# Windowed attention and MoE in one kernel: the first four head pairs turn their probabilities on TensorE, and the weight chunks arrive in the order of their use

## The chip, the cores and the metric

The kernel runs on one core of a Trainium2 chip. The metric is the device time of one execution in microseconds (us), the median of the runs. The engines are TensorE (PE; PEld is its weight load), VectorE (DVE), ScalarE (ACT), GpSimd (POOL) and SyncE (SP). DMAs are issued by SP, and after the change one by ACT too. A sequencer takes the instructions of its engine in program order.

## What is computed

Eight batches of eight heads with 512 local and 32 global tokens of head size 64. Local queries see the global keys and a band of keys around them; global queries see all 544 keys. The attention output, as 4608 tokens of 512 numbers, goes through one MoE layer:

```python
s_ll = scale * np.matmul(q_l, k_l.transpose(0, 1, 3, 2))
mask = np.abs(pos[:, None] - pos[None, :]) <= 32
s_l = np.concatenate([s_lg, np.where(mask, s_ll, -1e9)], axis=-1)
out_l = np.matmul(sm(s_l), np.concatenate([v_g, v_l], axis=2))
...
x = attn_out.transpose(0, 2, 1, 3).reshape(B * S, H * D)
h = np.maximum(x @ w_in, 0.0)
out = h * h @ w_out
```

## The kernel before

**Blocks and steps.** Tokens are worked on in 17 blocks of 256: 16 of local tokens, two for each batch, and a last one that holds all the global tokens. The MoE of a block takes eight steps; step m multiplies the block with 256 columns of the first weight (`gemm1`, line 380, two column halves j, each adding up four chunks of 128 rows), applies ReLU and square (`act1`, line 397, and `act2`), and multiplies the result with the 256 matching rows of the second weight (`gemm2`, line 424), one step later. The two PSUM tiles of `gemm1`, h0 and h1, have one buffer each, so the product of the next step cannot write h0 before `act1` has read it.

**Block 0 is special.** Its products run in plain float32 (two passes for each product on TensorE) on the weights as they come; from block 1 on, weights and tokens are split into a high and a low float32r part.

**Attention.** The local attention of a block is done in four head pairs s. For each pair: `scores` (line 146; sixteen products of 32 queries on 128 keys, into the two PSUM tiles sb), `softmax1` (line 201; four DVE instructions that add the mask and take the extreme), `softmax2` (line 219; four exponentials on ACT), `softmax3` (line 227; sums, reciprocal and scaling on DVE), `transposes` (line 233; one DVE instruction that transposes 32x32 squares), `av` (line 238; 40 products over 32 keys each, since the squares stay in their quadrant of partitions), and `x_evac` (line 263; copies into the tokens x, or xg for block 0). Every second pair, `g_scores` and `g_rest` do the scores of the global queries; the last copies them from sb to SBUF.

**The order** is written out by hand. Lines 542 to 595 are the prologue: loads, then the pairs 0 to 3 of block 0 and the scores of pair 4. The loop at line 596 then runs one MoE step and half a pair at a time. Products named `warm` (line 161) work on zeros, between the others. The prologue's loads go through one SP queue, with up to eight in flight.

**Weights.** They come as 32 chunks of 512 KB (`w_load`), as 64-bit floats, and are turned into float32 on the chip: `w_abs` on ACT (letter a, `w_first`), `w_shift` and `w_or` on DVE (letters b and c), and later the split, `w_split` on ACT and `w_low` on DVE (letter s). The table `PLAN` says with these letters what is done at the four places of each step; `w_need` (line 520) fills in what a step needs and the table has not done. Chunks 4m and 4m+1 belong to `gemm1` of step m, 4m+2 and 4m+3 to its `gemm2`. `LOOK` says how many chunks ahead a load is asked for. All chunks and the early loads of pairs share a pool of 33 buffers.

Of the kernel before, what the change touches and what calls it, by code (L numbers as in the profile page):

```python
# [16 lines left out]
P = 128  # L17
# [18 lines left out]
PLAN = [",,,", ",,,", ",,,", ",,,", ",,,", ",,,", ",,,", ",,,", "bca,bca,bca,bc", "a,abcbc,abc,abc", "as,abcbc,abc,abcs", "a,abcbc,abc,abcs", "as,abcbc,abc,abcs", "a,abcbc,abc,abcs", "aas,bc,bcs,bcss", "s,ss,ss,ss", "s,,s,ss", ",,s,s", "s,,s,", ",,s,s", "s,,s,", ",,s,s", "s,,s,s", ",,,"]  # L36
LOOK = 6
NFIRST = 5
VFIRST = 5
# [25 lines left out]
def attention_moe(  # L65
# [3 lines left out]
    vv: bass.AP,  # L69
    qg: bass.AP,  # L70
# [12 lines left out]
    p1 = ctx.enter_context(tc.tile_pool(name="p1", bufs=1))  # L83
    ps_h = ctx.enter_context(tc.tile_pool(name="ps_h", bufs=1, space=PSUM))
# [22 lines left out]
    def load_v(p):  # L107
        v = early(p, VC, "v") if p < VFIRST else pv.tile([P, 2, VC], F32, tag="v", name=f"v{p}")
        sp.dma_start(v, vv[p])
        pairs[p]["v"] = v  # L110
# [3 lines left out]
    def g_load(k):  # L114

        qr = p2.tile([P, P], F32, tag="qr", name=f"qr{k}")
        sp.dma_start(qr, qg[k // 4, k % 2])
        state["q", k] = qr
# [42 lines left out]
    def warm(n):  # L161
        h = ps_o.tile([P, 512], F32, tag="o0", name="warm") if "warm" not in state else state["warm"]
        state["warm"] = h
        z = sg[:, :, 544:]
        for _ in range(n):
            pe.matmul(h[:96, :192], z[:, 0], z, start=True, stop=True, skip_group_check=True)
# [70 lines left out]

    def av(p):
# [24 lines left out]
    def x_evac(p):  # L263
# [4 lines left out]
        if g == 0:  # L268
            ac.copy(xg[:, c, :64], v_at(0))
            ve.tensor_copy(out=xg[:, c, 64:128], in_=v_at(1))  # L270
            ac.copy(xg[:, c, 128:], src)
        else:
            xv = p2.tile([P, 2, 64], F32, tag="xv", name=f"xv{p}")
            ac.copy(xv[:, 0], v_at(0))
            ve.tensor_copy(out=xv[:, 1], in_=v_at(1))
            xh, xl = x[:, g % 2, c, 0], x[:, g % 2, c, 1]
            xv = xv.rearrange("p a n -> p (a n)")
            for cols, part in ((slice(0, 128), xv), (slice(128, 256), src)):
                ac.copy(xh[:, cols], part)
                ve.tensor_sub(xl[:, cols], part, f(xh[:, cols]))  # L280
# [91 lines left out]

    def win(ws, step, j, c):
        o = 256 * (c % 2) + 128 * j
        return ws[4 * step + c // 2][:, o : o + 128]

    def wout(ws, step, j):
        return ws[4 * step + 2 + j]
# [141 lines left out]
    def w_need(m):  # L520

        if m <= 8:
            while w_next["or"] < min(4 * m + 2, WCH):
                w_second()
                w_third()
        if 8 <= m < 16:
            while w_next["low"] < 4 * (m - 8) + 4:
                n = w_next["low"]
                w_chunk(True)
                assert w_next["low"] > n, (m, w_next, w_bufs, sorted(w_used)[-1:])  # L530

    def w_done(m):
        w_used.update(range(4 * m, 4 * m + 4))
        for i in (4 * m, 4 * m + 2):
# [18 lines left out]
    load_v(2)  # L553
    load_qk(4)
    w_fetch(3)
    load_v(3)
    sp.dma_start(con[:, 2 * SW :], consts[:, 2 * SW :])
    w_fetch(4)
    g_load(2)
    w_fetch(5)  # L560
    load_qk(5)
    w_fetch(6)
# [12 lines left out]
    warm(3)  # L575
    g_rest(1)
    for s in range(1, 4):
        softmax1(s)
        softmax2(s, 0)
        softmax2(s, 1)  # L580
        scores(s + 1)
# [175 lines left out]
```

## Time and profile before

| | us |
|---|---|
| median of three runs (lowest, highest) | 960.55 (960.12, 961.61) |
| the profiled execution, its own time | 959.55 |
| span of its profile, first to last instruction | 957.8 |
| TensorE busy in it | 937.4 (98%) |

The profile's times count from the first instruction. A row of the timeline has start, length, engine, line, operation, the tiles as out<-in, shapes and a count of merged instructions; in square brackets stands how long the engine had been idle, and what ended that. All instructions go through one helper, so that the line is always L58 and rows are told apart by their tiles. TensorE's float32 products show as two passes each.

### The profile page before, as it was taken

Reading aid. Unit: us, or ns where it says so; the run is one execution under the profiler, and the core shown is the slowest. Engines: PE = TensorE matmul, PEld = TensorE weight load, DVE = VectorE, ACT = ScalarE, POOL = GpSimd, SP = SyncE. Lnnn points to the kernel's source line nnn. Section 1 sums busy time; section 2 is a strip of 40 time slices with the busy share of each in tenths; the row PEclk is TensorE's granted clock in tenths of the full one; section 3 lists DMA queues with packets and bytes.
Section 4 is the critical chain, followed back from the end, with each engine's and each line's share of the span. In section 5 each row is a group of like instructions: output and inputs, shape, how many; then the busy total and the mean of one; then the engine's idle time right before and its main releaser. Section 6 shows DMA issues by size and latency. Waiting matters only on the chain.

```text
span 957.8 us, 28465 instructions
## 1 busy us (share of the span) xinstructions
PE 937.4 (98%) x12214; PEld 757.4 (79%) x12214; DVE 568.9 (59%) x1676; ACT 415.4 (43%) x1323; POOL 0.5 (0%) x5
## 2 busy tenths in 40 slices
PE   6999999999999999999999999999999999999997
PEld 4666688888888888888888888888888888888886
DVE  4578875655556655665556655565555655664442
ACT  4477644443344434444344434444444434433222
POOL 0000000000000000000000000000000000000000
PEclk9799999999999999999999999999999999999999
DMA  9891322233122312233222322233232223210000
GB/s 358 338 338 58 124 61 79 74 102 122 61 95 75 111 61 91 73 102 115 69 96 73 92 77 94 74 102 96 87 95 73 83 85 95 70 31 24 1 23 23
DMA packets 60191, 93.40 MB, mean 98 GB/s; under 512 B 10401, under 2 KB 35233, under 8 KB 60065
## 3 DMA queue, kind: packets, MB, share of 16 engines
q1 hardware_dynamic: 60064, 91.58, 28.8%
q8 instruction: 96, 1.57, 0.7%
q14 instruction: 31, 0.25, 0.1%
HBM read 82.12 MB, written 8.91 MB: 95 GB/s over the span
## 4 chain that ended last, share of the span: by engine, by line
PE 92%; ACT 3%; DVE 3%; issue 1%; DMA 1%; SPq 0%; ACTq 0%
PE h L58 40%; PE o L58 38%; PE sb L58 5%; PE ab L58 4%; PE va L58 4%; DVE wf L58 1%; ACT wf L58 1%; ACT r L58 1%; DVE ws L58 1%; DMA wr<-in_w_dram 1%; ACT prob L58 1%; DVE prob L58 0%; PE warm L58 0%; ACT ws L58 0%; ACT sg L58 0%
## 5 line engine op out<-in xcount | busy, mean ns | idle before, releaser
L58 PE MATMUL h<-x,ws 128*128 128x512 f32 (+1 forms) x2048 | 389.6, 343 | 2.3 <-DVE x L58 2.1
L58 PEld LDWEIGHTS h<-x,ws 128*128 128x128 f32 x2048 | 315.4, 188 | 61.0 <-ACT x L58 6.5
L58 PE MATMUL o<-ws,gh 128*128 128x512 f32 x1024 | 321.2, 395 | 0.0
L58 PEld LDWEIGHTS o<-ws,gh 128*128 128x128 f32 x1024 | 183.8, 188 | 39.7
L58 DVE TENSOR_TENSOR r<-h,r 128x256 f32<-128x256 f32 x256 | 106.9, 419 | 169.1 <-ACT r L58 169.1
L58 PE MATMUL o<-ws,gl 128*128 128x512 f32 x512 | 202.4, 395 | 0.0
L58 ACT COPY r<-h 128x256 f32<-128x256 f32 x256 | 94.7, 371 | 241.9 <-PE h L58 241.8
L58 DVE TENSOR_TENSOR gl<-r,gh 128x512 fp32r<-128x512 f32 x128 | 88.7, 693 | 87.8 <-ACT gh L58 87.8
L58 ACT CAST gh<-r 128x512 fp32r<-128x512 f32 x128 | 79.4, 620 | 113.1 <-DVE r L58 113.1
L58 PEld LDWEIGHTS o<-ws,gl 128*128 128x128 f32 x512 | 96.4, 188 | 22.6 <-DVE gl L58 0.2
L58 ACT ACTIVATE prob<-prob,st 128x128 f32<-128x128 f32 x256 | 100.5, 396 | 12.3 <-DVE st L58 12.2
L58 DVE SCALAR_TENSOR_TENSOR r<-r 128x512 f32<-128x512 f32 x128 | 88.5, 692 | 4.4
L58 PEld LDWEIGHTS va<-pts,v 32*64 32x64 f32 x2560 | 59.6, 133 | 27.4 <-issue 24.2
L58 PE MATMUL ab<-pts,v 32*64 32x64 f32 (+1 forms) x2560 | 69.2, 230 | 0.0
L58 PE MATMUL va<-pts,v 32*64 32x64 f32 (+1 forms) x2560 | 66.7, 229 | 2.4 <-issue 1.8
L58 DVE CUSTOM_DVE_ANT_0 prob<-sb,con 128x128 f32<-128x128 f32 x256 | 58.5, 284 | 8.2 <-PE sb L58 5.2
L58 PEld LDWEIGHTS ab<-pts,v 32*64 32x64 f32 x2560 | 58.5, 133 | 0.0
L58 ACT COPY xv<-va 128x64 f32<-128x64 f32 x60 | 12.7, 212 | 83.9 <-PE va L58 82.1
L58 ACT ACTIVATION_READ_ACCUMULATOR prob<-prob,st 128x1 f32 x256 | 48.6, 190 | 0.0
L58 PE MATMUL sb<-raw 64*32 64x128 f32 x2048 | 44.1, 278 | 3.8 <-DMA raw<-in_qk_dram 1.5
L58 DVE STREAM_TRANSPOSE pts<-prob 128x512 f32<-128x512 f32 x64 | 45.5, 711 | 2.5
L58 DVE TENSOR_TENSOR prob<-prob,st 128x512 f32<-128x512 f32 x64 | 44.3, 692 | 2.2
(50 smaller groups left out, 544.7 us busy)
## 6 DMA issues: line engine op xcount, KB each, us to landing
raw<-in_qk_dram SPq DMA_DIRECT2D x64, 480.0 KB, 4.9
v<-in_vv_dram SPq DMA_DIRECT2D x64, 320.0 KB, 3.6
wr<-in_w_dram SPq DMA_DIRECT2D x32, 512.0 KB, 8.7
gv<-in_vg_dram SPq DMA_DIRECT2D x32, 320.0 KB, 3.5
out_dram<-ot SPq DMA_DIRECT2D x32, 256.0 KB, 2.0
qr<-in_qg_dram SPq DMA_DIRECT2D x32, 64.0 KB, 4.9
xg<-xt SPq DMA_DIRECT2D x128, 4.0 KB, 1.8
out_dram<-ot SPq DMA_DIRECT2D x8, 64.0 KB, 1.7
```

What stands on the lines that cost most here:

```text
L58: r = method(*args, **kwargs)
```

## The change

**First four pairs.** Pairs 0 to 3 (`NTURN = 4`) no longer use `transposes`, `av` and `x_evac`. `turn` lets TensorE transpose the four 128x128 tiles of probabilities, by products with the identity, into one PSUM tile pt; `turn_evac` copies it to SBUF, one half on ACT and one on DVE; `turn_av` makes 16 products over 128 keys each, into h0 for even pairs and h1 for odd ones; `turn_x` copies the result on ACT. For that, the values of these pairs come in another layout (v1, 512 KB for each pair instead of 320 KB), in which the 128 partitions hold the 128 keys. The branch of `x_evac` for block 0 goes.

**Order of the phases.** The prologue is rewritten: the softmax of a pair starts before the one before it is scaled, the four pairs overlap, `g_scores(1)` comes late, and the scores of pair 4 and `g_scores(3)` stand behind the first `gemm1` instead of ahead of it. The value products of pair 3 stand right ahead of the first `gemm1`.

**Loads.** The first half of the masks is issued by ACT; the identity has a DMA of its own and comes early; two of the first weight chunks come later than before, the second half of the masks too. The query tiles of the global tokens get four buffers.

**Weights.** The chunks lie in memory in the order in which the steps use them (chunks 0 and 1 for `gemm1` of step 0, 2 and 3 for that of step 1, then the two of `gemm2` of step 0, and so on), `PLAN` has other letters in steps 8, 9, 14 and 15, `w_need` is asked ahead of each of the two products, and `LOOK` is 9 instead of 6.

```diff
-LOOK = 6
+LOOK = 9
+NTURN = 4
...
+    def turn(p):
+        if p == 0:
+            state["pt"] = ps_o.tile([P, 512], F32, tag="o1", name="pt")
+        for n in range(4):
+            pe.transpose(state["pt"][:, SW * n : SW * n + SW], probs[p % 2][:, n], ident)
+
+    def turn_evac(p):
+        pts = p1.tile([P, 4 * SW + 96], F32, tag="pts", name=f"pts{p}")
+        ac.copy(pts[:, : 2 * SW], state["pt"][:, : 2 * SW])
+        ve.tensor_copy(out=pts[:, 2 * SW : 4 * SW], in_=state["pt"][:, 2 * SW :])
+        pairs[p]["pts"] = pts
+
+    def turn_av(p):
+        d = pairs[p]
+        state["vt"] = ps_h.tile([P, 512], F32, tag=f"h{p % 2}", name=f"vt{p}")
+        for a in range(4):
+            for u in range(2):
+                for e in range(2):
+                    q = SW * (2 * e + u) + BLK * a
+                    o = 2 * BLK * a + BLK * u
+                    pe.matmul(
+                        state["vt"][half(e), o : o + BLK],
+                        d["v"][:, 2 * a + u, e],
+                        d["pts"][:, q : q + BLK],
...
+    def turn_x(p):
+        w_take(-1)
+        ac.copy(xg[:, p], state["vt"][:, :HALF])
...
+    def w_in(step):
+        return max(4 * step - 2, 0)
+
+    def w_out(step):
+        return min(4 * step + 4, WCH - 2)
...
+    ac.dma_start(masks[:, : 2 * SW], consts[:, : 2 * SW])
     load_qk(0)
-    sp.dma_start(masks[:, : 2 * SW], consts[:, : 2 * SW])
-    g_load(0)
     load_qk(1)
-    w_fetch(1)
     load_qk(2)
     load_v(0)
-    g_load(1)
+    sp.dma_start(ident, consts[:, 4 * SW :])
     load_qk(3)
-    w_fetch(2)
+    w_fetch(1)
+    g_load(0)
     load_v(1)
     load_v(2)
+    w_fetch(2)
+    load_v(3)
+    w_fetch(4)
     load_qk(4)
...
-    warm(4)
+    warm(16, 64)
     scores(0)
-    g_scores(0)
-    warm(2)
     softmax1(0)
     softmax2(0, 0)
     softmax2(0, 1)
+    warm(4)
     scores(1)
+    softmax1(1)
+    softmax3(0)
+    softmax2(1, 0)
+    softmax2(1, 1)
+    warm(1)
+    scores(2)
+    turn(0)
+    softmax1(2)
+    turn_evac(0)
+    softmax2(2, 0)
+    softmax2(2, 1)
+    turn_av(0)
+    softmax3(1)
+    scores(3)
     g_scores(1)
+    turn_x(0)
+    turn(1)
+    softmax1(3)
     w_first()
+    turn_evac(1)
+    softmax2(3, 0)
+    softmax2(3, 1)
...
+    softmax3(3)
+    turn(3)
+    turn_x(2)
+    w_first()
+    turn_evac(3)
+    warm(1)
+    w_third()
+    w_second()
+    w_third()
...
+        if t == LAG:
+            turn_av(s - 1)
+            turn_x(s - 1)
+            g_rest(1)
...
             gemm1(m, 0)
             gemm1(m, 1)
         run_jobs(t, "evac")
+        if t == LAG:
+            scores(s)
+            g_scores(s - 1)
+            w_tick(t, 0)
...
+        if m > 0:
+            w_need(m, 2)
```

On DVE, in the stretch where pair 1 is turned before the change: st and prob are the softmax's sums and probabilities, wf and wr weight chunks, xg the tokens of block 0, sb the scores.

```order
L58 TENSOR_SCALAR st_201<-st_201 128x4 [waits Activation_49]
L58 RECIPROCAL st_201<-st_201 128x4 [waits DVE_49]
L58 TENSOR_TENSOR prob_87<-prob_87,st_201 128x512 [waits DVE_49]
L58 STREAM_TRANSPOSE pts_320<-prob_87 128x512 [waits DVE_49,PE_49]
L58 TENSOR_SCALAR wf_194<-wf_194 128x512 [waits Activation_49]
L58 COPY xg<-va_1_324 128x64 [waits PE_49]
L58 SCALAR_TENSOR_TENSOR wf_194<-wr_109,wf_194 128x512 [waits DMAHW1_49,DVE_49]
```

On DVE after the change, from the copy of pair 1's transposed tile on, pairs 2 and 3 included (pt is the PSUM tile that TensorE transposes into):

```order
L59 COPY pts_306<-pt 128x256 [waits Activation_49]
L59 TENSOR_SCALAR st_238<-st_238 128x4
L59 RECIPROCAL st_238<-st_238 128x4 [waits DVE_49]
L59 TENSOR_TENSOR prob_89<-prob_89,st_238 128x512 [waits DVE_49]
L59 TENSOR_SCALAR wf_304<-wf_304 128x512
L59 COPY pts_340<-pt 128x256 [waits Activation_49]
L59 TENSOR_SCALAR st_299<-st_299 128x4
L59 RECIPROCAL st_299<-st_299 128x4 [waits DVE_49]
L59 TENSOR_TENSOR prob_90<-prob_90,st_299 128x512 [waits DVE_49]
L59 COPY pts_370<-pt 128x256 [waits Activation_49]
L59 SCALAR_TENSOR_TENSOR wf_304<-wr_107,wf_304 128x512 [waits DMAHW7_49]
```

The square transposes and the 64-column copies are gone, a copy of half of pt stands in their place and waits for ACT's copy of the other half, and the weight chunks' work has moved behind the pairs.

On ACT before the change, from the exponentials of pair 3 (x4) to the ReLU of the first product (r<-h):

```order
L58 ACTIVATE prob_87,st_376<-prob_87,st_376 128x128 x4
L58 COPY xg<-va_0_408 128x64
L58 COPY xg<-ab 128x128
L58 ACTIVATE wf_374<-wr_122 128x512
L58 COPY xg<-va_0_461 128x64
L58 COPY xg<-ab 128x128
L58 ACTIVATE prob_86,st_516<-prob_86,st_516 128x128 x2
L58 ACTIVATE wf_529<-wr_126 128x512
L58 ACTIVATE wf_529<-wr_130 128x512
L58 ACTIVATE r_536<-h_0_506 128x256
L58 ACTIVATE r_536<-h_1_511 128x256
```

On ACT after the change, from the last copies of the pairs to the same ReLU (sg holds the scores of the global queries, prob_89 the pair 4):

```order
L59 COPY pts_370<-pt 128x256
L59 COPY xg<-vt_377 128x256
L59 COPY sg<-sb_91 128x160
L59 COPY sg<-sb_92 128x128
L59 ACTIVATE wf_431<-wr_119 128x512
L59 ACTIVATE wf_431<-wr_121 128x512
L59 COPY sg<-sb_91 128x160
L59 COPY sg<-sb_92 128x128
L59 ACTIVATE prob_89,st_438<-prob_89,st_438 128x128 x2
L59 ACTIVATE wf_457<-wr_126 128x512
L59 ACTIVATE wf_457<-wr_128 128x512
L59 ACTIVATE r_466<-h_0_397 128x256
```

Between the last copy into xg and the ReLU there stood two exponentials and two weight chunks; now there are four copies of global scores, four chunks and the two exponentials, and the last two copies and the exponentials belong to scores that TensorE makes behind the first product.

More of the change, by code (lines that the diff above doesn't have):

```diff
@@ L69, in attention_moe @@
     vv: bass.AP,
+    v1: bass.AP,
     qg: bass.AP,
@@ L107, in load_v @@
     def load_v(p):
+        if p < NTURN:
+            w_take(1)
+            r = wp.tile([P, 1024], F32, tag="w", name=f"v{p}")
+            sp.dma_start(r, v1[p])
+            pairs[p]["v"] = r.rearrange("p (w e n) -> p w e n", w=8, e=2)
+            return
         v = early(p, VC, "v") if p < VFIRST else pv.tile([P, 2, VC], F32, tag="v", name=f"v{p}")
@@ L114, in g_load @@
     def g_load(k):
-        qr = p2.tile([P, P], F32, tag="qr", name=f"qr{k}")
+        qr = p4.tile([P, P], F32, tag="qr", name=f"qr{k}")
         sp.dma_start(qr, qg[k // 4, k % 2])
@@ L236, in transposes @@
         pairs[p]["pts"] = pts
+    def turn(p):
[20 more added lines that the diff above has]
+                        d["pts"][:, q : q + BLK],
+                        start=True,
+                        stop=True,
+                        skip_group_check=True,
+                    )
+    def turn_x(p):
+        w_take(-1)
+        ac.copy(xg[:, p], state["vt"][:, :HALF])
+        pairs[p]["v"] = None
     def av(p):
@@ L267, in x_evac @@
         src = ab[:, 448:576]
[L268 to L280, printed above, removed]
+        xv = p2.tile([P, 2, 64], F32, tag="xv", name=f"xv{p}")
+        ac.copy(xv[:, 0], v_at(0))
+        ve.tensor_copy(out=xv[:, 1], in_=v_at(1))
+        xh, xl = x[:, g % 2, c, 0], x[:, g % 2, c, 1]
+        xv = xv.rearrange("p a n -> p (a n)")
+        for cols, part in ((slice(0, 128), xv), (slice(128, 256), src)):
+            ac.copy(xh[:, cols], part)
+            ve.tensor_sub(xl[:, cols], part, f(xh[:, cols]))
         pairs[p]["v"] = None
@@ L571, in attention_moe @@
     softmax2(0, 1)
+    warm(4)
     scores(1)
+    softmax1(1)
[12 more added lines that the diff above has]
+    scores(3)
     g_scores(1)
+    turn_x(0)
+    turn(1)
+    softmax1(3)
     w_first()
[L575 to L581, printed above, removed]
-        g_scores(s + 1)
-        warm(1)
-        softmax3(s - 1)
-        transposes(s - 1)
-        w_second()
-        new_va(s)
-        av(s - 1)
-        x_evac(s - 1)
-        warm(3 if s < 3 else 1)
-        w_third()
-        g_rest(s + 1)
-        w_first()
-    softmax3(3)
-    transposes(3)
+    turn_evac(1)
+    softmax2(3, 0)
+    softmax2(3, 1)
+    warm(1)
+    turn_av(1)
+    softmax3(2)
+    turn(2)
+    turn_x(1)
+    w_second()
+    turn_evac(2)
+    warm(1)
+    turn_av(2)
+    softmax3(3)
+    turn(3)
+    turn_x(2)
+    w_first()
+    turn_evac(3)
+    warm(1)
+    w_third()
+    w_second()
+    w_third()
     for t in range(LAG, NSTEP + LAG + 1):
@@ L713 @@
             vv[:, hf, :, BLK * a : BLK * a + BLK, 4] = v_g
+    v1 = np.zeros((NTURN, P, 8, 2, D), f4)
+    for p in range(NTURN):
+        for a in range(4):
+            for u in range(2):
+                for slot in range(4):
+                    n = order[u][SHIFT[a] + slot]
+                    rows = slice(BLK * slot, BLK * slot + BLK)
+                    src = v_g if n == g else vb[:, :, u + n]
+                    v1[p, rows, 2 * a + u] = src[0, 2 * p : 2 * p + 2].transpose(1, 0, 2)
+    v1 = v1.reshape(NTURN, P, 16 * D)
     qk = np.ascontiguousarray(qk.reshape(NP, 2, P, QK).transpose(0, 2, 1, 3))
```

71 lines of the change are left out of this document (42 added, 29 removed).

## Prediction

> **What bounds the kernel now.** I read the page first, then the windows of the first 100 us, the timeline of TensorE there, the DMA queues, and for durations the groups of instructions.
>
> ```profile
> span 957.8 us, 28465 instructions
> PE 937.4 (98%) x12214; PEld 757.4 (79%) x12214; DVE 568.9 (59%) x1676; ACT 415.4 (43%) x1323; POOL 0.5 (0%) x5
> ...
> PEclk9799999999999999999999999999999999999999
> ```
>
> TensorE is busy for 98%, so only its early gaps, its early half clock and the moment when its dense work begins are left to win. The timeline of TensorE has them (here the rows of the big products and the long gaps):
>
> ```profile
> 1.04 2.87 PE L58 MATMUL warm<-sg 128*96 128x192 f32 x8 [1.04 <-POOL sg L138]
> ...
> 7.08 0.67 PE L58 MATMUL sb<-raw 64*32 64x128 f32 x32 [1.21 <-DMA raw<-in_qk_dram]
> 7.51 0.55 PE L58 MATMUL sb<-raw,qr 64*32 64x160 f32 x16
> ...
> 16.15 0.55 PE L58 MATMUL sb<-raw 64*32 64x128 f32 x23 [1.24 <-issue]
> ...
> 22.45 2.08 PE L58 MATMUL warm<-sg 128*96 128x192 f32 x6 [3.82 <-issue]
> ...
> 32.47 8.57 PE L58 MATMUL h<-xg,wf 128*128 128x256 f32 x32
> ...
> 46.34 3.72 PE L58 MATMUL h<-xg,wf 128*128 128x256 f32 x16
> ...
> 55.72 2.86 PE L58 MATMUL h<-xg,wf 128*128 128x256 f32 x12 [1.33 <-DVE wf L58]
> ...
> 72.38 2.86 PE L58 MATMUL h<-xg,wf 128*128 128x256 f32 x12 [0.25 <-DVE wf L58]
> ...
> 97.59 1.32 PE L58 MATMUL h<-x,ws 128*128 128x512 f32 x6
> 101.02 2.02 PE L58 MATMUL h<-x,ws 128*128 128x512 f32 x10 [2.11 <-DVE x L58]
> ```
>
> Dense work begins at 32.47 with the first two `gemm1` (32 passes), which end at 41.04. From there on TensorE is held up by three gaps of note, 1.33 + 0.25 + 2.11 = 3.7 us, the last in the first product of block 1, which starts at 97.59; all later work is the same before and after. So the end moves by two terms: how much earlier the second `gemm1` ends, and how much of the 3.7 us goes.
>
> Why does it begin only at 32.47? The windows tell:
>
> ```profile
> 16.10:18.70 2.60, 2.48 (x127) 2.00 (x128) 0.70 (x3) 0.17 (x2) 0.00 (x0) 1.00 1.06 398
> ...
> 18.70:21.60 2.90, 0.00 (x0) 0.02 (x1) 2.73 (x14) 2.71 (x13) 0.00 (x0) 1.00 1.02 398
> 21.80:35.20 13.40, 10.84 (x209) 8.03 (x209) 5.97 (x21) 3.51 (x11) 0.00 (x0) 0.50 1.03 404
> ```
>
> Counts up to the first gap, and DVE's work on the way to block 1:
>
> ```profile
> 0.00:15.50 15.50, 10.79 (x221) 7.70 (x221) 6.36 (x34) 8.07 (x31) 0.46 (x5) 1.00 0.89 335
> ...
> 28.60:97.60 69.00, 65.22 (x791) 44.10 (x790) 54.24 (x142) 46.10 (x121) 0.00 (x0) 0.95 0.61 228
> ```
>
> The queue of instruction fetches, in the window of 19 to 21 us and over the run (packets, MB, share):
>
> ```profile
> q8 instruction: 1, 0.02, 3.5%
> ...
> q8 instruction: 96, 1.57, 0.7%
> ```
>
> The columns of the windows are PE, PEld, DVE, ACT, POOL, the granted clock, the DMA share and GB/s. In the gap of 18.7 to 21.6 TensorE waits for nothing but "issue", with all DMA engines full. Between that gap and the one of 1.24 us it had issued 127 + 128 = 255 instructions. One packet of code came in 19 to 21 us; over the run 96 packets carry 1.57 MB, 16 KB each. So I read it that TensorE ran dry: its code arrives in blocks of about 256 instructions, behind a full queue of data. The Trainium skill (Runtime: NRT & Kernel Launch, section Instruction fetch mechanics) has the same 16 KiB blocks but calls the fetch hidden. By the page the change would win 1.0 us more than in the sum below; the gaps of 1.24 and 3.82 us here speak against it. After the long gap the clock stays at 0.50 until 35.3, and the first two products take 8.57 us instead of 2 x 3.72.
>
> **The change, term 1: when the second `gemm1` ends.** Durations first. From the chain of waits in order of time (start, length, what):
>
> ```profile
> 2.60 5.58 DMA wr<-in_w_dram
> ...
> 9.08 0.29 DVE prob L58
> ...
> 10.34 0.70 DVE prob L58
> 11.07 0.72 DVE pts L58
> 11.84 0.27 PE va L58
> ```
>
> The first and last row of pair 0's four exponentials on ACT:
>
> ```profile
> 5.49 0.40 ACT L58 ACTIVATE prob<-prob,st 128x128 f32<-128x128 f32 x1 [3.48 <-DVE st L58]
> ...
> 6.95 0.18 ACT L58 ACTIVATION_READ_ACCUMULATOR prob<-prob,st 128x1 f32 x1
> ```
>
> From the groups by form (count, busy us and mean ns), the nearest relatives of what is new, and a weight chunk's three steps:
>
> ```profile
> L58 ACT COPY r<-h 128x256 f32<-128x256 f32 x256 | 94.7, 371 | 241.9 <-PE h L58 241.8
> L58 DVE TENSOR_TENSOR r<-h,r 128x256 f32<-128x256 f32 x256 | 106.9, 419 | 169.1 <-ACT r L58 169.1
> L58 DVE COPY gp<-ab 128x128 f32<-128x128 f32 x1 | 0.3, 285 | 0.0
> L58 PE MATMUL ab<-con,sg 128*128 128x128 f32 x5 | 0.7, 273 | 0.0
> L58 PE MATMUL ab<-gv,gp 128*32 128x64 f32 x40 | 0.8, 222 | 0.0
> L58 ACT ACTIVATE wf<-wr 128x512 f32<-128x512 f32 x32 | 20.2, 667 | 1.1 <-DMA wr<-in_w_dram 1.1
> L58 DVE TENSOR_SCALAR wf<-wf 128x512 int32<-128x512 int32 x32 | 13.3, 415 | 10.0 <-ACT wf L58 10.0
> L58 DVE SCALAR_TENSOR_TENSOR wf<-wr,wf 128x512 int32<-128x512 int32 x32 | 22.2, 695 | 1.0
> ```
>
> A `softmax1` takes 0.9 us (9.08 to about 10.0), `softmax3` 1.1 us (to 11.05), a pair's exponentials 1.65 us (5.49 to 7.13). A turn is four transposes like the five of 0.7 us: 0.65. ACT's half of `turn_evac` is the 371 ns copy. DVE's half is shown by no row: between the 285 ns of half its size and the 419 ns of an add from PSUM I take 0.42, near the row of its own size. The value products, 32 passes over 128 keys, come nearest to the 40 passes of 0.8 us: 0.6; if every pass waited for a weight load, at the product's 3.72/16 = 0.23 us, they would be 7 us, which the products' 256 columns against 32 here speak against, so 1.7 at most. Loads: the first weight chunk landed at 8.18 with 1.70 MB up to it, 4.2 us at 404 GB/s, so a load lands 4.0 us after its bytes' time. In the new order that gives pair 1's queries and keys at 6.8, pair 2's at 8.0, values of pair 0 at 9.3 and of pair 3 at 17.3, the identity at 9.4, weight chunks 0 and 1 at 12.0 and 16.0. The larger values (192 KB more a pair) and the masks on ACT's queue are in these sums; no load ends up last.
>
> Step by step: the 32 small warm passes, a third of the 0.36 us row each, end at about 4.8, so the first scores (0.67 us each time) at 5.5. Pair 1's scores follow at 7.1 to 7.8, its `softmax1` at 7.9 to 8.8, pair 0's `softmax3` behind it on DVE until 9.9, `turn(0)` until 10.6. `softmax1(2)` writes the tile that is being turned, so it ends at 11.3, and DVE's half of `turn_evac(0)`, queued behind it, at 11.75; value products, scores 3 and `g_scores(1)` take TensorE to 13.45. Here its second wait for code falls. Counting four instructions a product and two a transpose, the 442 (221 + 221) that ran before the first gap are used up at the end of `g_scores(1)`. The next block is asked for in `scores(1)` at 7.4; after the gaps above it ran 6.3 us after the block before it had started (16.15 to 22.45), the first one 8.2 us (8.0 to 16.15). That gives 13.7 to 15.6: a wait of 0.2 to 2.2 us, I take 1.0. The block after that is asked for at 14.5 and needed at 26.
>
> From `turn(1)` at 14.5 the pairs run in a chain, each: turn 0.65, ACT's copy 0.4, then DVE's copy 0.42 (it waits for ACT's), `softmax3` of the next pair 1.1, handoffs 0.25, about 2.8 us; so `turn(2)` at 17.4, `turn(3)` at 20.15, its copies done at 21.7, its value products at 22.35. The first `gemm1` begins at 22.4 with chunk 0; chunk 1 is shifted and joined behind the last copy on DVE (0.61 + 0.43 + 0.61 of pitch) until 23.35, so the product ends at 26.15.
>
> Then a new wait. The scores of pair 4 and `g_scores(3)` hold TensorE to 27.3 (1.1 us that before lay ahead of 32.47). The second `gemm1` writes h0 and must wait for ACT's ReLU; and that is queued behind the copies of the global scores, which wait for `softmax1(4)` (27.75), two exponentials (28.85) and two weight chunks (29.95). It starts at 30.3 and ends at 34.0, against 41.04: **7.0 us**. Before, the clock's 1.2 us and the late start hid that queue.
>
> **Term 2: the gaps.** The two on wf came as DVE had not joined chunks in time. In the new order `gemm1` of step m needs 4m chunks, not 4m + 2, two chunks or 2.1 us of DVE less. The 2.11 us at 98.9 came as DVE joined the last two chunks ahead of the tokens of block 1; `PLAN` now does them in step 7. From 23.4 until block 1 begins, at about 89.6 (97.6 - 7.0 less 1.0 of gaps), DVE has 66 us for the 54.2 us of work that it did between 28.6 and 97.6. Asking nine chunks ahead keeps DMA full until about 67 us (25.1 MB up to the last chunk), where it was 0.61 busy on average. I keep 0.7 of the 3.7 us: **3.0 us**.
>
> Together 10.0 us: 959.55 becomes 949.5. The median of before lies 1.0 above its profiled execution, so I forecast 950.5. The bounds: no wait for code (-0.8), no gaps (-0.7), DVE's copies at 0.29 (-0.4), shorter queue on ACT (-0.8), first scores sooner (-0.3) make 947.5; the block of code late (+1.2), value products at 1.7 (+1.1 on the path, twice), half of the gaps back (+1.5) make 955.4.
>
> **Rivals.**
>
> *The clock drops* (0.2). TensorE's pairs have many short pauses and one of 3.0 us behind the first product. Before, the clock fell 3.0 us after the idle time began, and 10.84 busy us of 13.40 did not bring it back while the matmuls were small. If it falls in the prologue, each pair's scores, turn and values grow by about 0.7, and the first two products cost the 1.2 us again: 4.0 us, 954.5. Against it: until the long gap the clock stayed at 1.00 with gaps of up to 1.24 us. The Trainium skill (TensorE: Matmul & The Clock Gate, Part 1) lets the clock fall after an idle window of 3.4 us that runs free and raises it after a busy one; by that, an estimate from the page, the pause alone would cost nothing or up to 1.7 us. The trace agrees on the fall (3.0 us into the gap) and not on the rise.
>
> *DVE and ACT cannot follow* (0.15). If they wait as much as before (69 us for 54 us of work), block 1 begins at 23.4 + 69 = 92.4, 5.2 us earlier than before and no more, with its own gap as it was: 955.3. For it speaks the chain DVE, ACT, DVE of each chunk; against it that chunks now come earlier.
>
> *Slower: TensorE runs out of code among the small products of the loop* (0.04). A pair's 64 small products (40 + 16 + 8) use a whole block of 256 in 2 us, while a block takes 6.3 us under a full queue, and the queue is now full until 67 us. Should two boundaries fall into the same pair, each time 4.1 us are lost; three such pairs of the four make 12.3 us, 962.8 with all gains spent. The point is where the boundaries lie: by my count 1210 and 1466 enclose pair 5 and 8 us of work, so it decides only if a block takes over 8 us. In before no such gap showed after 32.47.
>
> *The code's wait only moves* (0.01): the first product would still come at 32, about 960.
>
> **How the numbers follow.** The forecast case has 0.60 and is 950.5, by itself 947.5 to 953; the range goes on to the rivals at 954.5 and 955.3 and the upper bound: 947.5 to 956. A measurement of this kernel can tell about 0.2% (1.9 us) from no change. Faster 0.95, same 0.01, slower 0.04.
>
> **What would show it.** Right: the first `gemm1` starting at 21.5 to 24 at clock 1.00; no "issue" gap over 2.2 us; a pause of about 3 us ahead of the second `gemm1`, ended by ACT's r; block 1's first product near 89.6 with under 1 us of gap. Wrong: a first product after 26, PEclk at 0.50 beyond 10 us, or gaps on wf or x that add up to 3.7 us again.

## The result, and the profile after

| | before | after |
|---|---|---|
| median of four runs each (lowest, highest), us | 960.34 (959.89, 961.61) | 949.40 (948.81, 950.44) |
| after / before, 95% interval | | 0.9885 (0.9868 to 0.9902) |
| profiled execution, its own time, us | 959.55 | 948.81 |
| end of the second `gemm1` | 41.03 | 35.37 |
| end of block 1's first product | 103.04 | 92.52 |
| end of TensorE's last product | 952.59 | 941.78 |

The changed kernel is 1.15% faster; 950.5 was forecast, 949.4 measured, inside the range. "Lead" below is how much earlier than before the same product ends: 5.66 us at the second `gemm1`, 10.53 at block 1's first product, 10.81 at the end. So the first term of the sum is 5.7 us (7.0 forecast) and the second 4.9 (3.0 forecast): the total holds because two misses, of 1.4 and 1.9 us, have opposite signs. That is luck.

The page of the changed kernel, in the lines that answer to those of before:

```profile
span 947.0 us, 28126 instructions
PE 933.7 (99%) x12048; PEld 756.3 (80%) x12048; DVE 567.2 (60%) x1672; ACT 416.5 (44%) x1323; POOL 0.5 (0%) x5
...
PEclk9999999999999999999999999999999999999999
```

The timeline of TensorE, in its rows with the turned pairs (pt: the transposes, vt: the value products) and the big products:

```profile
9.93 0.63 PE L59 MATMUL pt<-con,prob 128*128 128x128 f32 x4 [0.40 <-ACT prob L59]
11.02 0.30 PE L59 MATMUL vt<-pts,v 128*64 128x32 f32 x2 [0.46 <-ACT pts L59]
11.59 1.12 PE L59 MATMUL vt<-pts,v 128*64 128x32 f32 x30 [0.27 <-DVE pts L59]
12.64 0.67 PE L59 MATMUL sb<-raw 64*32 64x128 f32 x32
13.10 0.53 PE L59 MATMUL sb<-raw,qr 64*32 64x160 f32 x16
13.56 0.66 PE L59 MATMUL pt<-con,prob 128*128 128x128 f32 x4
...
16.30 0.66 PE L59 MATMUL pt<-con,prob 128*128 128x128 f32 x4
...
18.92 0.66 PE L59 MATMUL pt<-con,prob 128*128 128x128 f32 x4
...
20.74 1.12 PE L59 MATMUL vt<-pts,v 128*64 128x32 f32 x30 [0.16 <-DVE pts L59]
21.79 3.72 PE L59 MATMUL h<-xg,wf 128*128 128x256 f32 x16
25.44 0.67 PE L59 MATMUL sb<-raw 64*32 64x128 f32 x32
25.90 0.53 PE L59 MATMUL sb<-raw,qr 64*32 64x160 f32 x16
29.97 5.41 PE L59 MATMUL h<-xg,wf 128*128 128x256 f32 x16 [3.53 <-ACT r L59]
35.21 3.60 PE L59 MATMUL o<-wf,r 128*128 128x512 f32 x8
```

No pause ends with "issue" any more; the first product begins at 21.79 in place of 32.47. Then come 3.53 us of pause, and a second product of 5.41 us where the first took 3.72. ACT's timeline shows what the second product waits for:

```profile
27.28 0.48 ACT L59 COPY sg<-sb 128x160 f32<-128x160 f32 x2 [3.52 <-DVE st L59]
27.66 0.40 ACT L59 ACTIVATE prob<-prob,st 128x128 f32<-128x128 f32 x1
...
28.44 1.20 ACT L59 ACTIVATE wf<-wr 128x512 f32<-128x512 f32 x2
29.55 0.64 ACT L59 ACTIVATE r<-h 128x256 f32<-128x256 f32 x2
```

The windows (PE, PEld, DVE, ACT, POOL, granted clock, DMA share, GB/s) show what the pause does to the clock, and TensorE without a gap behind it:

```profile
21.80:26.40 4.60, 4.60 (x66) 3.62 (x64) 2.70 (x5) 1.86 (x5) 0.00 (x0) 1.00 1.03 398
26.40:30.00 3.60, 0.07 (x3) 0.04 (x1) 1.78 (x10) 2.72 (x10) 0.00 (x0) 1.00 1.04 399
...
31.40:34.80 3.40, 3.40 (x10) 2.64 (x9) 2.46 (x6) 2.17 (x6) 0.00 (x0) 0.50 1.03 410
40.00:100.00 60.00, 60.00 (x638) 40.69 (x623) 52.28 (x140) 44.53 (x118) 0.00 (x0) 1.00 0.62 225
```

The ReLU stands at 29.55, behind the copies of the global scores, two exponentials and two weight chunks. Of the 3.6 us TensorE works 0.07; the clock is at half from 31.37 to 34.78, a stretch of 3.41 us. From 40 to 100 us TensorE is busy for 60.00 of 60.00, so the gaps of the second term are gone to the last one.

### The profile page after: what moved, and what is told of

It reads as the page before. It is cut to its first block, busy times and chain, and to the rows that moved or that the text cites. A ratio compares the mean times of both kernels' runs of the same rounds, so it can differ in the third digit from the quotient of the medians.

```text
span 947.0 us, 28126 instructions
## 1 busy us (share of the span) xinstructions
PE 933.7 (99%) x12048; PEld 756.3 (80%) x12048; DVE 567.2 (60%) x1672; ACT 416.5 (44%) x1323; POOL 0.5 (0%) x5
## 4 chain that ended last, share of the span: by engine, by line
PE 98%; ACT 1%; DVE 0%; DMA 0%; issue 0%; ACTq 0%
PE h L59 43%; PE o L59 41%; PE sb L59 5%; PE ab L59 4%; PE va L59 4%; PE vt L59 0%; DMA raw<-in_qk_dram 0%; DVE prob L59 0%; ACT prob L59 0%; ACT wf L59 0%; DVE pts L59 0%; PE warm L59 0%; PE pt L59 0%; ACT pts L59 0%; ACT ot L59 0%
## 5 line engine op out<-in xcount | busy, mean ns | idle before, releaser
L59 PEld LDWEIGHTS o<-ws,gl 128*128 128x128 f32 x512 | 96.3, 188 | 22.4 <-DVE gl L59 0.2
L59 PEld LDWEIGHTS va<-pts,v 32*64 32x64 f32 x2400 | 55.0, 130 | 23.7 <-issue 21.5
L59 PE MATMUL ab<-pts,v 32*64 32x64 f32 (+1 forms) x2400 | 64.1, 227 | 0.0
L59 PE MATMUL va<-pts,v 32*64 32x64 f32 (+1 forms) x2400 | 61.6, 226 | 0.0
L59 PEld LDWEIGHTS ab<-pts,v 32*64 32x64 f32 x2400 | 54.0, 130 | 0.0
L59 DVE STREAM_TRANSPOSE pts<-prob 128x512 f32<-128x512 f32 x60 | 42.7, 712 | 2.0
```

Source lines behind the costliest of these rows:

```text
L59: r = method(*args, **kwargs)
```

## The experiments

Twelve more kernels ran. All times are in us; each was timed beside runs of the kernel before on its chip (medians there 959.35 to 960.28). The two last columns come from the profiled execution: the lead over before at the end of the second `gemm1`, and how much it grows until block 1's first product has ended.

| kernel | median (lowest, highest) | to before, 95% interval | lead | growth |
|---|---|---|---|---|
| after | 949.40 (948.81, 950.44) | 0.9885 (0.9868, 0.9902) | 5.66 | 4.87 |
| relu_first | 947.17 (946.21, 952.01) | 0.9872 (0.9851, 0.9893) | 4.92 | 2.72 |
| warm_fill | 949.02 (948.34, 949.95) | 0.9885 (0.9872, 0.9899) | 6.10 | 4.14 |
| relu_warm | 946.92 (946.35, 947.52) | 0.9869 (0.9854, 0.9885) | 10.04 | 2.76 |
| relu_warm_low | 945.23 (944.96, 945.92) | 0.9853 (0.9829, 0.9877) | 10.36 | 3.75 |
| old_chunks | 950.89 (950.80, 951.10) | 0.9905 (0.9891, 0.9918) | 4.10 | 4.87 |
| look6 | 950.94 (949.11, 951.88) | 0.9910 (0.9895, 0.9926) | 3.24 | 4.85 |
| old_plan | 956.78 (954.10, 962.20) | 0.9973 (0.9954, 0.9992) | 0.67 | 1.39 |
| plan_only | 954.76 (950.99, 955.31) | 0.9944 (0.9927, 0.9961) | -0.71 | 5.01 |
| weights_only | 954.98 (952.96, 955.91) | 0.9949 (0.9936, 0.9963) | 1.58 | 5.06 |
| old_turning | 956.56 (955.12, 957.42) | 0.9967 (0.9953, 0.9980) | -0.76 | 3.14 |
| old_turn | 956.54 (955.38, 957.18) | 0.9964 (0.9951, 0.9977) | -1.57 | 4.30 |
| fewer_warm | 959.69 (958.16, 960.08) | 1.0005 (0.9990, 1.0020) | 0.75 | -1.55 |

### What the pause costs: the queue on ACT, and the clock

**relu_first** moves the ReLU in the loop's first step:

```diff
         if t == LAG:
             scores(s)
             g_scores(s - 1)
             w_tick(t, 0)
+            act1(m)
         if now:
             softmax1(s)
...
-        if run:
+        if run and t > LAG:
             act1(m)
```

> The changed kernel with one move: in the step behind the first gemm1, act1 stands ahead of softmax1, g_rest and the exponentials on ACT, so that ACT's ReLU is the first thing behind the product. Theory 1 (the pause of 3.53 us at 26.43 is ACT's queue, and the clock of 0.50 from 31.37 to 34.78 is that pause's doing): no gap above 1 us ahead of the second gemm1, which then begins at about 27 and takes 3.72 us instead of 5.41; 2.5 to 3.5 us of pause and 1.7 us of clock go, less up to 1.5 us that the next gemm2 or gemm1 may wait for chunks 4 and 5, which DVE now joins no earlier: 3 to 5 us faster than the changed kernel, 944.5 to 946.5 us, and the second gemm1 ends at about 31 instead of 35.38. Rival a (the weight chunks are the limit there, the ReLU only happens to be last): the wait turns into one on wf of the same size, the time stays within 1 us of the changed kernel. Rival b (the clock falls for another reason than the pause, the prologue's many short gaps): a stretch of 0.50 stays somewhere before 40 us and only 2 to 3 us are won.

The pause is gone: the second product follows the first by 0.9 us of scores. But the profiled execution, 952.01, lost the clock much earlier. Its windows, and its big products in the timeline:

```profile
8.40:11.80 3.40, 1.89 (x41) 1.18 (x40) 2.88 (x19) 2.66 (x13) 0.00 (x0) 1.00 1.05 407
11.80:15.20 3.40, 3.40 (x79) 2.85 (x79) 0.87 (x2) 1.83 (x8) 0.00 (x0) 0.51 1.02 407
15.20:28.90 13.70, 13.70 (x122) 11.50 (x120) 6.72 (x23) 5.82 (x19) 0.00 (x0) 0.50 1.03 402
```

```profile
26.78 4.75 PE L59 MATMUL h<-xg,wf 128*128 128x256 f32 x16
32.39 3.72 PE L59 MATMUL h<-xg,wf 128*128 128x256 f32 x16
```

A stretch with 1.5 us of short pauses lowered the clock, and the 15 us from 11.84 on in which TensorE was busy without a break, but mostly with small products, did not bring it back; it came back at 28.91, within the first `gemm1`. In warm_fill and look6, whose prologue is the same, one such stretch did (15.34 and 16.55), so the kind of products alone does not decide it. That is the prediction's rival "the clock drops", in one execution of five. The four others took 946.2 to 947.5; the median is 2.2 us under the changed kernel's. So theory 1 holds as to the pause, but the saving is below its 3 to 5, and rival b holds too, now and then. This profile can't show that the later half clock was the pause's doing; warm_fill and relu_warm can.

**warm_fill** fills the pause in the same step:

```diff
             g_scores(s - 1)
+            warm(8)
             w_tick(t, 0)
```

> The changed kernel with eight more warm products on zeros behind g_scores(3), in the pause ahead of the second gemm1; nothing else moves, and ACT's ReLU ends where it did. Theory 1 (the pause lets the clock fall): the second gemm1 still begins at about 30, but at clock 1.00, and takes 3.7 us instead of 5.41: 1.7 us faster than the changed kernel, about 947.7 us. Rival (the clock falls through the small products and short pauses of the prologue, or through something else that the warm products don't touch): the stretch of 0.50 is still there, and the time is that of the changed kernel within 0.5 us. If the warm products at half clock last beyond the ReLU, up to 1 us slower.

```profile
23.03 3.72 PE L59 MATMUL h<-xg,wf 128*128 128x256 f32 x16
27.60 2.84 PE L59 MATMUL warm<-sg 128*96 128x192 f32 x16
31.21 3.72 PE L59 MATMUL h<-xg,wf 128*128 128x256 f32 x16 [0.77 <-ACT r L59]
...
56.63 3.69 PE L59 MATMUL h<-xg,wf 128*128 128x256 f32 x16 [0.73 <-ACT x L59]
```

The second product takes 3.72 again: with the pause filled the clock stays, so the 1.7 us were the pause's. The median is only 0.4 us lower, though, which is the rival's time (within 0.5) and not theory 1's 947.7. In the profiled execution the clock was at half from 11.93 to 15.34, which put the first product 1.24 us later, and a new wait of 0.73 us came at 55.90: together more than the 1.69 saved, and at the end of block 1's first product its lead is 0.29 us smaller than the changed kernel's. The one execution that shows a mean clock of 1.00 took 948.34, still only 0.5 us under the fastest of the changed kernel. The mechanism is shown, the saving is not.

**relu_warm** is relu_first with three more warm products:

```diff
-    warm(1)
+    warm(2)
     scores(2)
+    warm(1)
     turn(0)
...
+    warm(1)
     turn_av(0)
```

> The kernel with act1 first, and three more warm products on zeros in the pauses of pair 0: one each ahead of scores(2), turn(0) and turn_av(0), where TensorE had idled 0.37, 0.40 and 0.46 us. With act1 first alone, the profiled execution lost the clock from 11.84 to 28.91, behind a stretch of 3.41 us with 1.5 us of such pauses, and was 952.01; the others were 946.2 to 947.5. Theory 4 (the clock falls after a stretch of 3.41 us with too little work, and it depends on where the stretches happen to lie): all executions stay near clock 1.00 until 30 us, no time over 948, median 945.5 to 947. Rival a (the clock falls for another reason): one execution in five is at 950 to 952 again, median about 947. Rival b (the warm products hold up pair 0): the whole prologue is 0.3 to 0.8 us later and the median 947 to 948.

```profile
22.70 3.72 PE L59 MATMUL h<-xg,wf 128*128 128x256 f32 x16
27.27 3.72 PE L59 MATMUL h<-xg,wf 128*128 128x256 f32 x16
31.34 3.67 PE L59 MATMUL o<-wf,r 128*128 128x512 f32 x8 [0.35 <-ACT prob L59]
```

```profile
86.24 1.32 PE L59 MATMUL h<-x,ws 128*128 128x512 f32 x6
88.23 2.01 PE L59 MATMUL h<-x,ws 128*128 128x512 f32 x10 [0.68 <-DVE x L59]
```

The profiled execution kept the clock through the prologue, and the others (946.35 to 947.52, mean clock 0.998 to 1.000) leave no room for a loss like that of relu_first (0.989). The lead at the second `gemm1` is 10.04: 4.4 more than in the changed kernel (3.53 of pause and 1.7 of clock, less 0.9 of a later first product). Yet the end gains only 2.5, since the growth falls from 4.87 to 2.76: TensorE now comes early enough to wait for ACT and DVE again, at 30.99 and at 87.55 above. These two make 1.0 of the 2.1 us; the rest was not followed.

**relu_warm_low** moves two letters:

```diff
-"as,bcs,bcs,ss", "s,,s,ss"
+"as,bcs,bcs,", "sss,,s,ss"
```

> The kernel with act1 first and three more warm products, and in PLAN the last two letters s of step 15 moved to the start of step 16, so that DVE copies the tokens of block 1 ahead of two splits of weights. There the first product of block 1 had waited 0.68 us for x. Theory (DVE's order ended that wait, and the table sets it): that gap goes, 0.6 to 1.0 us faster, 945.7 to 946.5 us. Rival (ACT's x is late anyway, or the splits are missed a step later): the wait stays or moves, 946.5 to 947.5 us.

```profile
26.96 3.72 PE L59 MATMUL h<-xg,wf 128*128 128x256 f32 x16
...
85.88 3.05 PE L59 MATMUL h<-x,ws 128*128 128x512 f32 x16
```

The wait for x is gone and the median is 945.23, a little below what was expected; the theory holds. This version is faster than both kernels: its slowest run, 945.92, lies 2.9 us under the fastest of the changed kernel.

### Which part of the weights' change closes the gaps

The change reorders the chunks, asks for them nine ahead, and has new letters in `PLAN`. **old_chunks** takes back the first, with the old `w_need` and the old indices of the chunks:

```diff
-        return max(4 * step - 2, 0)
+        return 4 * step
...
-        return min(4 * step + 4, WCH - 2)
+        return 4 * step + 2
```

> The changed kernel with the chunks in the old order (0 to 3 for step 0, 4 to 7 for step 1 and so on) and the old w_need; LOOK 9, the turning, the phases and the letters of PLAN stay. Theory 1 (the gaps on wf in the loop went because gemm1 of step m needs two chunks fewer, the lead between the ends of step 1 and step 8 grew by 4.9 us for that): the gap on wf near 48 is back, and as DVE must join two chunks more ahead of the second gemm1, that waits too; 1.5 to 5 us slower than the changed kernel, 951 to 954.5 us. Rival (the gaps went because loads are asked for nine ahead, or because everything began earlier with DVE free): the gaps stay away, within 1 us of the changed kernel.

**weights_only** is the kernel before with all three, and with that part of the change's diff alone (the lines of the new `PLAN` and of the new order are not shown):

```diff
-LOOK = 6
+LOOK = 9
...
-            w_need(m)
+            w_need(m, 1)
...
+        if m > 0:
+            w_need(m, 2)
```

> The kernel before, with the new order of chunks, the new w_need, the new letters of PLAN and LOOK 9; prologue and turning are as before. Theory 1 (the two parts of the change add up, and this is the second): the prologue keeps its two issue gaps and the clock of 0.50, the second gemm1 ends at 41 within 1 us, the gaps on wf at 54 and 72 and the one on x at 98.9 are gone: 3 to 5 us faster than before, about 956 us. Rival a (the gaps went only because the new prologue leaves DVE free earlier): at least 2 us of gaps stay, and the win is under 2 us. Rival b (nine chunks asked ahead fill the queue, and the block of code comes later still): the gap of 3.82 us grows by the time of the loads that now lie ahead of it, and the time is that of before or worse.

**look6** is the changed kernel with the old distance:

```diff
-LOOK = 9
+LOOK = 6
```

> The changed kernel with LOOK = 6, so that loads of chunks are asked for six ahead as before. With the old order of the chunks the gaps stayed away, so order is not what removes them. Theory 2 (the table PLAN removes them: it lets ACT and DVE do two chunks more in its first step, and the loads were early enough already): no gap over 0.3 us between 40 and 95 us, the time of the changed kernel within 1 us, 948.5 to 950.5 us. Rival (asking nine ahead removes them, because the table can only do what has landed): gaps on wf of 1 to 2 us come back, and the lead over the kernel before stays near 5.7 us: 952 to 954 us.

**plan_only** is the kernel before with the new table (steps 8, 9, 14 and 15 differ):

```diff
-"bca,bca,bca,bc", "a,abcbc,abc,abc"
+"abcabc,abcabc,a,", "bca,bca,bca,bca"
...
-"aas,bc,bcs,bcss", "s,ss,ss,ss"
+"aas,abcbc,abcs,bcss", "as,bcs,bcs,ss"
```

> The kernel before with nothing but the new letters of PLAN; order of the chunks, w_need, LOOK 6, prologue and turning are as before. Theory 2 (the table alone is the second term): the gaps of 1.33 us at 54.40 and of 2.11 us at 98.91 go, and the time falls by the 5 us that the new order, the table and LOOK 9 together gave: 954 to 956 us. Rival a (LOOK 9 is needed): the gap at 54.40 stays, only the one of 2.11 us, which two late joins cause, goes: 957 to 958 us. Rival b (letters that find no landed chunk hold up ACT or DVE ahead of the ReLU): the time is that of before or up to 2 us worse.

The column "growth" answers: 4.87 with the old order, 4.85 with six ahead, 5.01 with the table alone, 5.06 with all three on the kernel before. None of these four has a gap on wf or x left from 40 us on. So the new table is enough for the second term, and with it in place the order of the chunks and `LOOK` add nothing that can be seen. On the kernel before, the table alone wins 4.6 us, and all three together 4.8. Theory 1, as it stood for old_chunks, falls as to the gaps of the loop, and theory 2 holds; the times of old_chunks and look6 (950.89 and 950.94) are half a us above what "within 1 us of the changed kernel" allows. The window of plan_only that answers to the one quoted of before (54.24 us of DVE, x142):

```profile
28.60:97.60 69.00, 67.18 (x800) 46.84 (x801) 57.00 (x156) 47.55 (x127) 0.00 (x0) 0.95 0.64 236
```

DVE does 14 instructions more in the same stretch: the old letters had left it idle with chunks landed, for 3.51 us at 36.5 alone. The smaller lead of old_chunks and look6 at the second `gemm1` is clock (that product took 6.33 and 6.56 us, and look6 had lost it once before) and, in old_chunks, a pause of 3.98 us that DVE's wf ended, in place of 3.53 by ACT's r, as theory 1 had said of this place. The two medians are 1.5 us above the changed kernel's, which is about the size of these.

**old_plan** is the reverse, the changed kernel with the old letters, the diff above with its signs turned.

> The changed kernel with the old letters of PLAN; new order of the chunks, w_need, LOOK 9, turning and phases stay. With the new letters alone the kernel before had won the whole second term. Theory 2 (the letters are needed, since they decide when ACT and DVE do the chunks): gaps on wf near 47 and 64 and on x near 93 come back, 3 to 5 us slower than the changed kernel: 952.5 to 954.5 us. Rival (in the new order a step needs two chunks fewer, so w_need has the slack that the letters gave; the two are alternatives): the gaps on wf stay away, only the wait for x at the start of block 1 is back, 1.5 to 2.3 us slower: 951 to 951.8 us.

```profile
94.40 1.98 PE L59 MATMUL o<-wf,r 128*128 128x512 f32 x4 [2.77 <-DVE wf L59]
103.96 4.24 PE L59 MATMUL o<-wf,r 128*128 128x512 f32 x6 [2.98 <-DVE wf L59]
```

The letters are needed, as theory 2 says, but it loses 7.4 us where 3 to 5 were expected, and at a place that neither theory named: in the new order the chunks that come last belong to `gemm2` of the last two steps, and the old letters had left them over. The gaps on wf that the kernel before has ahead of `gemm1` stay away here, as the rival said: the new order and the nine loads ahead, which are not separated here, close those without the new letters, and the shortage moves to `gemm2`. The second gap lies behind the end of the column "growth", and so does a stretch of half clock from 103.39 to 106.80. The profiled execution (962.03) also had the clock at half from 11.23 to 31.71; the median, 956.78, has less of that.

### What wins the prologue, and where the waits for code went

**old_turning** keeps the changed kernel's phases and loads (the values in the old layout) and goes back to DVE's transposes, the 40 value products and the three copies, the transposes at the place of `turn_evac`:

```diff
     def turn(p):
-        if p == 0:
...
+        pass
...
     def turn_evac(p):
...
+        transposes(p)
...
     def turn_av(p):
...
+        new_va(p)
+        av(p)
```

> The changed kernel with its order of phases and of loads, but pairs 0 to 3 go by the old transposes on DVE, 40 value products over 32 keys, and copies on ACT and DVE. Theory 3 (the first term comes from the order of the phases and from the smaller queue of loads ahead of the code; TensorE's turning only takes work off DVE): a pair costs DVE about 0.7 us more for the transposes in the place of 0.42 for a copy, plus a copy of the values, and TensorE 0.8 in place of 0.6 + 1.2: first gemm1 at 22 to 24, the time within 1.5 us of the changed kernel, 949 to 951 us. Rival (the turning is what lets the pairs follow each other): the period of a pair grows by 1 us or more, the first gemm1 comes at 25 to 27, 952 to 955 us.

At that place softmax1 of pairs 2 and 3 has overwritten what pairs 0 and 1 should transpose, so it doesn't compute the attention, and its order on DVE is not the one that was meant. Its first `gemm1` begins at 27.08 and its time, 956.56, lies beyond both forecasts. **old_turn** mends it:

```diff
     def turn(p):
-        pass
+        transposes(p)
...
     def turn_evac(p):
-        transposes(p)
+        pass
```

> The changed kernel with its order of phases and of loads, but pairs 0 to 3 go by DVE's transposes at the place of turn, the 40 value products over 32 keys, and copies of the tokens on ACT and DVE. In old_turning the transposes stood behind softmax1 of the next pair but one, which overwrites what they read; here they stand ahead of it. Theory 3 (TensorE's turning and the shorter value products are what lets the pairs follow each other and keeps the code short: 36 passes a pair in the place of 80): TensorE issues 88 more instructions a pair, so pauses without a named releaser are back between 15 and 21 us, 1 to 4 us in sum; the first gemm1 at 24.5 to 27, the time 952 to 956 us. Rival (the order of phases and the loads bring the first term): first gemm1 within 1.5 us of 21.8, no such pause over 0.5 us, 949 to 951 us.

Its long pauses on TensorE's timeline:

```profile
13.38 0.89 PE L59 MATMUL sb<-raw 64*32 64x128 f32 x23 [1.28 <-issue]
19.69 0.40 PE L59 MATMUL warm<-sg 128*96 128x192 f32 x1 [1.99 <-issue]
26.12 0.37 PE L59 MATMUL ab<-pts,v 32*64 32x64 f32 x3 [2.88 <-issue]
37.19 5.41 PE L59 MATMUL h<-xg,wf 128*128 128x256 f32 x16 [3.53 <-ACT r L59]
```

The waits for code are back, 6.15 us of them, and the new pause on ACT's r on top: the first `gemm1` begins at 27.11 and the whole first term is lost (lead -1.57). It is slower than theory 3 forecast (27.11 for 24.5 to 27, 956.54 for 952 to 956, 6.15 us of waits for 1 to 4), and the clock was at half from 10.54 to 17.36 and from 20.77 to 31.02; but the rival, a first product within 1.5 us of 21.79, falls. So theory 3 of this run holds: the order of phases alone wins nothing here. Whether the turning alone, in the old order, would win the term was not run, and how much of the 5.3 us is code and how much DVE's longer work is not separated.

The two runs also show that a pause does not always cost the clock. In old_turning a pause of the same 3.53 us was followed by a product at full clock:

```profile
38.07 3.72 PE L59 MATMUL h<-xg,wf 128*128 128x256 f32 x16 [3.53 <-ACT r L59]
```

The clock changes only at the ends of stretches of 3.41 us. In old_turning the pause lay in two of them with 1.69 and 1.84 us, and the clock stayed; with 0.77 and 2.76 us in old_turn, and 1.53 and 2.00 in the changed kernel, it fell.

**fewer_warm** puts the reading of those waits as code to the test in the kernel before:

```diff
-    warm(2)
     softmax1(0)
...
-    warm(3)
     g_rest(1)
...
-        warm(1)
+        if s > 1:
+            warm(1)
...
-        warm(3 if s < 3 else 1)
+        if s > 1:
+            warm(3 if s < 3 else 1)
```

> The kernel before without nine of its warm products in the prologue, all ahead of the first long gap (18 passes, so 36 instructions of TensorE with their weight loads); the computation is whole. Theory 5 (the two gaps of 1.24 and 3.82 us are TensorE out of code, at a fixed count of instructions): the first gap stands behind 442 instructions again, and so 18 passes later in the program, behind pass 21 of the 32 of scores(3) where it stood behind pass 3; the second behind 698 again, among the first passes of scores(4) where it stood in the warm products ahead of them. TensorE comes there sooner, and the block not, so the sum of the two gaps is 4 to 7 us. Rival (a wait for data or for a semaphore that the trace does not name): the gaps stay at the same places of the program. The time is a by-product: 957 to 963 us.

```profile
15.19 1.74 PE L58 MATMUL sb<-raw 64*32 64x128 f32 x27 [1.48 <-DVE st L58]
...
23.29 0.63 PE L58 MATMUL sb<-raw 64*32 64x128 f32 x21 [0.90 <-issue]
28.17 0.28 PE L58 MATMUL va<-pts,v 32*64 32x64 f32 x4 [2.23 <-issue]
29.58 0.26 PE L58 MATMUL va<-pts,v 32*64 32x64 f32 x1 [0.96 <-issue]
```

Not every row that ends with "issue" is a wait for code: the one at 28.17 ends 0.10 us after DVE's transposes of that pair (27.36, 0.71 us long), which it must wait for; the one at 29.58 comes in the middle of the value products. The kernel before has such a row of DVE's too, 1.84 us at 30.63, 0.11 us after the transposes; the prediction does not list it.

```profile
27.36 0.71 DVE L58 STREAM_TRANSPOSE pts<-prob 128x512 f32<-128x512 f32 x1
```

The second wait for code now stands behind 11 of the 32 passes of `scores(4)`, where it stood ahead of the six warm passes before them; counted from the start it is behind 347 passes, and 348 before. It has moved in the program by the passes that are gone and stayed where it was in the count. The first one has all but gone: TensorE reached the 221st pass only at 16.04, after other pauses, and the block had landed at 15.10. The next pass begins at 16.47, 1.37 us after the landing, where its neighbours begin 0.01 us apart; as the pass ahead lasts until then at half clock, the profile shows no pause. So the waits for code sum to 1.9 us (0.90 + 0.96), or up to 2.3 with that one, not 4 to 7; the other pauses and half a clock took the time instead, and the whole is as long as before. Theory 5 holds as to the place, not as to the sum; the rival falls.

Counting TensorE's passes in all these traces gives the rest. Waits for code stand behind 221 passes in before, weights_only, plan_only and old_turn, behind 347 to 349 in these and in old_turning and fewer_warm, and a third behind 474 to 476 in old_turn, old_turning and fewer_warm. Behind 728 and 729 passes, in the loop, old_turn and old_turning wait once more (0.49 and 1.58 us). One packet of 16 KB on the queue of instructions lands 4.4 to 6.9 us after pass 94 and the next 4.2 to 5.6 us after pass 221, the starts of the block before (all fourteen traces), and where TensorE waits, it goes on 1.2 to 1.5 us after the landing (before: landed 14.76 and 21.01, on at 16.15 and 22.45). In the changed kernel the packets land at 11.85 and 18.64, and TensorE comes to pass 221 at 13.31 and to pass 349 only at 24.48: with 36 passes a pair in place of 80 its code lasts longer than a block takes. The first of the two is close: in relu_warm_low the block came too late, and TensorE waited 0.34 us behind 221 passes.

## Why the prediction was right, point by point

- **What bounds it** held: early gaps, early clock and the start of the dense work were all that moved.
- **The start of the pairs**: `scores(0)` at 5.04 for 5.5, `turn(1)` at 13.56 for 14.5. The step that failed here is "I take 1.0" for the wait for code. The place was right (pass 221 falls into the last passes of `g_scores(1)`, at 13.31); the block came sooner. It landed at 11.85, so could run from about 13.3 (1.4 later), 5.9 us after pass 94 at 7.39, where I had taken 6.3 to 8.2. Measured 0, below my lower end of 0.2.
- **The chain of the pairs**: 2.74 and 2.62 us from turn to turn, 2.8 forecast. In it, turns of 0.66 for 0.65, ACT's copy 0.37, DVE's 0.42 as taken. The value products take 1.05 us (11.59 to 12.64 for the last 30), not 0.6; the bound of 1.7 held. The relatives, 40 passes in 0.8 us, had been too cheap by three quarters. The first `gemm1` began at 21.79, forecast 22.4: 1.0 of code less, half a us of value products more.
- **The new pause**: forecast, with its cause, at 3.0 us, measured 3.53, as the scores ended at 26.43 in place of 27.3, 0.87 us sooner, while ACT's queue ended only 0.40 sooner (29.55 for 29.95). relu_first shows the cause.
- **The clock**: the sum had no term for it, and it took 1.7 us (5.41 for 3.72). The prediction had it in a rival's sentence, "the pause alone ... up to 1.7 us", from the Trainium skill (TensorE: Matmul & The Clock Gate, Part 1). Here that was the whole amount; warm_fill shows that filling the pause keeps the clock, old_turning that the amount depends on where the pause lies. This is what made the first term 5.7 and not 7.0: the second `gemm1` began 0.33 earlier than forecast and took 1.69 longer.
- **The second term**: 4.9 for 3.0. "I keep 0.7" failed, the gaps went completely, and another of 0.30 us at 89.45 that I had not listed. Each of the three gaps on wf also cost 0.26 to 0.30 us more than its idle time: step 3's product took 5.25 us before and 3.62 after, at a gap of 1.33. The reasons given hold in part. The letters alone close all gaps (plan_only). The order of use with nine loads ahead does take the gaps from `gemm1`, but without the letters others come at `gemm2` (old_plan), and with them it adds nothing that can be seen.
- **The rivals**: the prologue did not lose the clock in the profiled execution, but those of relu_first, warm_fill, look6 and old_plan, with the same prologue, did: for one stretch in two of them, for five and six in the others. The price of 4.0 us fits the long losses (relu_first: 952.01 against 946.21 to 947.45). That none came in the changed kernel's profile is partly luck, and 0.2 was rather low. DVE and ACT did follow (52.28 and 44.53 us of work in 60), and became the bound only when the pause was taken away. In the changed kernel TensorE did not run out of code in the loop; old_turn and old_turning show that it can.

What stays open: why the block lands after 4.4 us in one trace and after 6.9 in another, and by what measure the clock judges a stretch. The busy share does not separate them: one with 0.64 busy kept the clock (before, from 14.84), one with 0.66 lost it (warm_fill, from 8.52).

## What to carry to other kernels

In a prologue with full DMA queues, count TensorE's instructions: replacing many small products by few larger ones can win less by their own time than by the code that need not be fetched. When a product is moved ahead of other work, look at once at what is queued in front of its reader on the next engine, and allow for the half clock behind a pause of over 3 us: 1.7 us here after 3.53, nothing in old_turning. And where a change has several parts, undo each alone: here a table of letters did what the reordering and the deeper queue seemed to do.

## What the runs showed of the hardware

- The clock changed only on a grid of 3.41 us in these traces: 31.37 and 34.78 in the changed kernel, 11.93 and 15.34 in warm_fill, 11.84 and 28.91 (five stretches) in relu_first. The Trainium skill (TensorE: Matmul & The Clock Gate, Part 1) has such a free-running window; the trace agrees. Its rule that an idle window lowers the clock and a busy one raises it is not all that these runs show: 1.5 us of pauses in 3.4 lowered it, and the small products from 11.84 to 26.78 in relu_first, with TensorE busy throughout, did not raise it, while the same products did in warm_fill, from 11.93 to 15.34.
- TensorE's code came in blocks of 16 KB, each good for some 127 passes with their weight loads, the first two landing 4.2 to 6.9 us after the block before had been begun, and usable 1.2 to 1.5 us later. The Trainium skill (Runtime: NRT & Kernel Launch, section Instruction fetch mechanics) has the block's size and calls the fetch mostly hidden; the trace of before, with 1.24 and 3.82 us of waits, does not agree while loads fill the DMA queues.
- Scatter: 944.96 to 945.92 in the four executions of relu_warm_low, 954.10 to 962.20 in twelve of old_plan, whose mean clocks fall from 0.997 to 0.988 as the times grow. Long pauses alone do not make scatter: old_turn, with 6.15 us of waits, stayed within 955.38 to 957.18 in twelve.
